# The first batch's q and k requested on GpSimd's queue instead of SyncE's, and zero fills cut to what is read

## The chip, the cores and the metric

The kernel runs on one core of a Trainium2 chip. The core has five engines that work side by side, each with its own instruction stream: TensorE (PE in the profile; its weight loads are listed apart as PEld), VectorE (DVE), ScalarE (ACT), GpSimd (POOL) and SyncE (SP), which only issues transfers here. DMA transfers are requested by an instruction on SP, ACT or POOL and then carried out by 16 DMA engines. In the profile, q1 is the queue of the requests from SP ("hardware_dynamic") and q0 that of the requests from POOL ("software_dynamic").

The metric is the time of one execution on the device in microseconds (us); the median of several runs counts. A profiled execution takes a little longer than an unprofiled one.

## The reference

There are 8 batches, each with 8 heads of 576 positions and 64 features. Linear attention with the feature map phi comes first, then an MLP mixer with a residual (token mixing, then channel mixing):

```
phi(x) = where(x > 0, x, exp(x) - 1) + 1
kv  = phi(k)^T v              (per head, 64 x 64)
z   = sum over positions of phi(k)
x   = phi(q) kv / (phi(q) z + 1e-6)          -> (8, 576, 512)
u   = x + (relu(x^T w_tok1) w_tok2)^T        w_tok1 576x256, w_tok2 256x576
out = u + relu(u w_ch1) w_ch2                w_ch1 512x1536, w_ch2 1536x512
```

All inputs and the output are float32; the kernel computes with bfloat16 operands and float32 sums.

## The kernel before, in words

**Tiling.** The 576 positions of a batch are seen as 64 rows of T = 9 positions. q, k and v of one batch lie on 128 partitions: two groups of 64 rows (heads in two sets), and each of the three tensors is loaded in two halves, `c` = 0 and 1, of two heads per group. One load is 576 KB (128 partitions x 2 x 576 float32). `load` (line 221) makes one such request; batch 1 goes through GpSimd's queue into buffers 1, all other batches through SP's queue into buffers 0. `load_v0` (line 227) loads batch 0's v with a cast to bfloat16 on the way, always on GpSimd's queue, into the space that later holds `cr[1]`.

**Order.** Nothing is left to a scheduler. Each piece of work is a function with a name in the table `tok`, and the long string `ORDER` says in which order the pieces are recorded; that fixes the order on each engine. Semaphores between the engines are derived from which buffers the pieces read and write. The program gives GpSimd's DMAs eight semaphores in turn, so that the ninth waits until the first has landed, and so on.

**The start.** Ahead of `ORDER` stand, from line 1093 on, some instructions that are recorded directly. They are what the change touches:

- DVE fills a zero block (`zeros`, which lies in batch 1's v buffer and feeds the warming matmuls of PE at line 1089) and a one-element tile; ACT runs one exponential on it.
- SP requests the four halves of batch 0's k and q, in the order k0, q0, q1, k1.
- GpSimd makes the identity matrix (for PE's transposes), then zeroes `w1t` (line 1107; the last token weights, of which a half of the partitions is loaded later) and `qT[0]` (line 1108), and requests the two halves of v (recorded at line 230).
- DVE zeroes `kvbd` (line 1106) and `qT[1]` (line 1109), and sets the column of ones in `vs`.
- GpSimd then fills the end of `w2p` (line 1112) and requests the weights: `w1` in two pieces (line 1130), `w1t` (1131), `w2` (1132) and the first two of four blocks of `wc1` (1118). From `ORDER` follow, still on GpSimd, batch 1's k, q and v among the rest of `wc1` and `wc2`.

`qT` holds the transposed phi(q) in blocks of 64 columns. Matrix products read 128 columns at a time from it, so that the last window of a group reaches over 64 columns behind the group's own data; those must hold something finite.

**Batch 0.** For each half: ACT takes the exponential (line 249), DVE x + 1 with a maximum (line 253) and then the minimum of both (line 259), which is phi. PE transposes phi(q) with the identity (line 317), ACT and DVE copy the result into `qT` (line 323), PE multiplies phi(k) with ones (line 561) and with v (line 570), then `qT` with the result (lines 585 and 592), DVE and ACT divide (lines 601 to 616), and PE goes on with the token weights (lines 624 and 635) and with the channel weights (line 683). Warming matmuls (line 1089) stand between the first of these.

**Handing over to batch 1.** Batch 1's v is cast to bfloat16, one half on ACT and one on DVE (line 272), and PE's product of phi(k) and v (line 299) waits for both. From there on the batches run one after another, overlapped, and SP requests the halves of later batches.

The lines that matter most, before the change:

```python
    def load(nm, n, c, gate=None):
        src_ = src[nm][n].rearrange("(j a) (p t) d -> (a p) j (t d)", a=2, t=T)
        js = slice(2 * c, 2 * c + 2)
        queue = nc.gpsimd if n == 1 else nc.sync
        return after(queue.dma_start(out=raw[nm, rb(n)][:, js], in_=src_[:, js]), gate)
```

Of the kernel before, what the change touches and what calls it, by code (L numbers as in the profile page):

```python
# [111 lines left out]
def kernel(  # L112
# [20 lines left out]
    nc = tc.nc  # L133

    B, H, S, D = q.shape
# [5 lines left out]
    T = 2 * R + 1  # L141
# [28 lines left out]
    def const(name, shape, dt=BF16):  # L170
        return consts.tile(shape, dt, name=name, tag=name)

    w1 = const("w1", [128, R, DTOK])
    w1t = const("w1t", [128, 2, DTOK])
# [10 lines left out]
    qT = [const(f"qT{b}", [128, (4 * T + 1) * D]) for b in range(2)]  # L185
# [27 lines left out]
    def after(ins, other):  # L213
        if other is not None:
            tc.add_manual_dep(ins.ins, other.ins.name, sync_dep, reason="order of transfers")
        return ins

    def rb(n):
        return 1 if n == 1 else 0

    def load(nm, n, c, gate=None):
        src_ = src[nm][n].rearrange("(j a) (p t) d -> (a p) j (t d)", a=2, t=T)
        js = slice(2 * c, 2 * c + 2)
        queue = nc.gpsimd if n == 1 else nc.sync
        return after(queue.dma_start(out=raw[nm, rb(n)][:, js], in_=src_[:, js]), gate)

    def load_v0(c):
        src_ = v[0].rearrange("(j a) (p t) d -> (a p) j (t d)", a=2, t=T)
        js = slice(2 * c, 2 * c + 2)
        nc.gpsimd.dma_start(out=v0[:, js].rearrange("p j t d -> p j (t d)"), in_=src_[:, js])  # L230
# [48 lines left out]
    def load_in(nm, n, c):  # L279
        gate = GATE.get(f"{n}{nm}{c}")  # L280
        live["in", nm, n, c] = load(nm, n, c, live[gate] if gate else None)
# [815 lines left out]
    for c, nms in enumerate(("kq", "qk")):  # L1097
        for nm in nms:
            tok[f"0L{nm}{c}"]()
    make_identity(nc, identity)  # L1100
    nc.vector.memset(ones, 0.0)
    for a in range(2):
# [1 line left out]
    nc.vector.memset(vs[:, :, :, D:D1], 1.0)  # L1104
    for b in range(2):
        nc.vector.memset(kvbd[b], 0.0)
    nc.gpsimd.memset(w1t, 0.0)
    nc.gpsimd.memset(qT[0], 0.0)
    nc.vector.memset(qT[1], 0.0)
    for c in range(2):  # L1110
        load_v0(c)
    nc.gpsimd.memset(w2p[:, NT * TD:], 0.0)
    NB = 4
    CB = DCH // NB
# [83 lines left out]
```

## Time and profile before

| | |
|---|---|
| median of 3 runs | 242.99 us (242.88 to 243.49) |
| the profiled execution | 244.04 us, of which the span (first to last instruction) is 242.3 us |
| PE busy | 233.3 us, 96% of the span |
| DVE, ACT, POOL busy | 88%, 56%, 33% |
| granted TensorE clock | 0.999 |
| read from memory, written | 35.85 MB, 9.44 MB |

The page of a profile gives first the busy time of each engine, then the span in 40 equal slices (each digit is the busy share of a slice in tenths), then the DMA queues, and then the chain of work that ended last, followed back from the last instruction. In a timeline row stand start, length, engine, line, operation, output and inputs, and in brackets how long the engine was idle before and what ended the wait. A wait for several semaphores is put down to the one that came last.

### The profile page before, as it was taken

Reading aid. Unit: us, or ns where it says so; the run is one execution under the profiler, and the core shown is the slowest. Engines: PE = TensorE matmul, PEld = TensorE weight load, DVE = VectorE, ACT = ScalarE, POOL = GpSimd, SP = SyncE. Lnnn points to the kernel's source line nnn. Section 1 sums busy time; section 2 is a strip of 40 time slices with the busy share of each in tenths; the row PEclk is TensorE's granted clock in tenths of the full one; section 3 lists DMA queues with packets and bytes.
Section 4 is the critical chain, followed back from the end, with each engine's and each line's share of the span. In section 5 each row is a group of like instructions: output and inputs, shape, how many; then the busy total and the mean of one; then the engine's idle time right before and its main releaser. Section 6 shows DMA issues by size and latency. Waiting matters only on the chain.

```text
span 242.3 us, 6371 instructions
## 1 busy us (share of the span) xinstructions
PE 233.3 (96%) x2616; PEld 174.4 (72%) x2616; DVE 214.0 (88%) x389; ACT 135.7 (56%) x224; POOL 80.8 (33%) x92
## 2 busy tenths in 40 slices
PE   7799999999999999999999999999999999999991
PEld 3485445465678678789777887788678868888880
DVE  5889986999999999999999999999999699867661
ACT  4764781678695287428993496548914442347000
POOL 8684306370800620046000620215014900440730
PEclk9999999999999999999999999999999999999999
DMA  6999999999799988897937989594971285143035
GB/s 237 267 204 302 314 296 303 410 171 307 263 291 175 327 208 156 293 160 259 301 108 162 379 270 182 88 294 156 157 141 25 45 176 108 24 103 70 3 91 170
DMA packets 49037, 48.42 MB, mean 200 GB/s; under 512 B 30064, under 2 KB 35568, under 8 KB 49008
## 3 DMA queue, kind: packets, MB, share of 16 engines
q1 hardware_dynamic: 40032, 31.46, 47.7%
q0 software_dynamic: 8336, 15.76, 28.7%
q10 hardware_dynamic: 640, 0.79, 1.0%
q8 instruction: 20, 0.33, 0.5%
q14 instruction: 9, 0.07, 0.1%
HBM read 35.85 MB, written 9.44 MB: 187 GB/s over the span
## 4 chain that ended last, share of the span: by engine, by line
PE 86%; DMA 8%; DVE 1%; ACT 1%; issue 1%; SPq 1%; ACTq 0%
PE ps L967 26%; PE ps L925 23%; PE ps L445 6%; PE ps L744 5%; DMA v_raw<-in_v_dram 5%; PE ps L456 4%; PE ps L683 4%; DMA k_raw<-in_k_dram 3%; PE ps L708 2%; PE ps L299 2%; PE ps L730 2%; PE ps L1021 2%; PE ps L384 2%; PE ps L624 1%; PE ps L635 1%
## 5 line engine op out<-in xcount | busy, mean ns | idle before, releaser
L967 PE MATMUL ps<-k_raw,v_raw 128*128 128x256 bf16 x252 | 31.5, 273 | 0.0
L940 ACT COPY v_raw<-ps 128x512 f32<-128x512 f32 x30 | 17.2, 593 | 24.1 <-PE ps L925 18.5
L967 PEld LDWEIGHTS <-cr 128*128 128x128 bf16 x252 | 24.5, 98 | 4.8
L967 PEld LDWEIGHTS <-v_raw 128*128 128x128 bf16 x252 | 24.2, 98 | 3.8 <-issue 0.4
L925 PEld LDWEIGHTS <-swc 128*128 128x128 bf16 x240 | 23.3, 98 | 3.5 <-issue 0.4
L925 PEld LDWEIGHTS <-wc 128*128 128x128 bf16 x216 | 21.1, 98 | 4.0
L678 DVE CUSTOM_DVE_ANT_0 cr<-ps,v_raw 128x512 bf16<-128x512 f32 x30 | 20.0, 683 | 4.3 <-PE ps L925 2.1
L925 PE MATMUL ps<-crt,swc 128*128 128x256 bf16 x180 | 23.4, 273 | 0.0
L249 ACT ACTIVATE e<-q_raw 128x1152 bf16<-128x1152 f32 x16 | 18.7, 1167 | 6.7 <-DMA q_raw<-in_q_dram 6.3
L683 PE MATMUL ps<-uT,wc 128*128 128x512 bf16 x96 | 21.9, 379 | 0.0
L967 PE MATMUL ps<-wc,cr 128*128 128x256 bf16 x168 | 21.6, 273 | 0.0
L1068 POOL TENSOR_TENSOR obuf<-obuf,w 128x512 f32<-128x512 f32 x6 | 7.8, 1294 | 40.3 <-DVE obuf L1061 20.2
L249 ACT ACTIVATE e<-k_raw 128x1152 bf16<-128x1152 f32 x16 | 18.6, 1166 | 3.9 <-DMA k_raw<-in_k_dram 3.9
L1068 POOL TENSOR_TENSOR obuf<-obuf,q_raw 128x512 f32<-128x512 f32 x6 | 8.2, 1374 | 35.6 <-DVE obuf L1061 35.6
L925 PE MATMUL ps<-uT,wc 128*128 128x256 bf16 x144 | 19.7, 273 | 0.0
L1061 DVE TENSOR_TENSOR obuf<-ps,u 128x512 f32<-128x512 f32 x24 | 16.3, 684 | 2.7 <-PE ps L967 2.4
L1068 POOL TENSOR_TENSOR obuf<-obuf,part 128x512 f32<-128x512 f32 x6 | 7.7, 1286 | 27.1 <-DVE obuf L1061 27.1
L410 DVE TENSOR_TENSOR x<-ps,dens 128x768 bf16<-128x768 f32 x18 | 16.5, 937 | 0.0
L683 PEld LDWEIGHTS <-wc 128*128 128x128 bf16 x96 | 9.1, 98 | 9.8
L467 DVE TENSOR_TENSOR u<-ps,x 128x1024 bf16<-128x1024 f32 x12 | 14.5, 1218 | 0.1
L833 DVE TENSOR_TENSOR v_raw<-cr 128x512 bf16<-128x512 bf16 (+3 forms) x24 | 14.5, 617 | 0.0
L445 PE MATMUL ps<-x,w 128*128 128x512 bf16 x56 | 14.4, 379 | 0.0
(172 smaller groups left out, 515.1 us busy)
## 6 DMA issues: line engine op xcount, KB each, us to landing
k_raw<-in_k_dram SPq DMA_DIRECT2D x14, 576.0 KB, 6.0
q_raw<-in_q_dram SPq DMA_DIRECT2D x14, 576.0 KB, 5.3
v_raw<-in_v_dram SPq DMA_DIRECT2D x12, 576.0 KB, 6.7
out_dram<-obuf POOLq DMA_DIRECT2D x12, 512.0 KB, 5.7
wc<-in_moe_w_ch_dram POOLq DMA_DIRECT2D x8, 384.0 KB, 11.7
k_raw<-in_k_dram POOLq DMA_DIRECT2D x2, 576.0 KB, 10.0
q_raw<-in_q_dram POOLq DMA_DIRECT2D x2, 576.0 KB, 12.1
v_raw<-in_v_dram POOLq DMA_DIRECT2D x2, 576.0 KB, 11.8
```

Source lines behind the costliest of these rows:

```text
L249: nc.scalar.activation(out=ebuf[EBUF[f"{n}{nm}{c}"]], in_=f, func=AF.Exp)
L410: nc.vector.tensor_tensor(out=xv[:, :, rc0:rc0 + 3], in0=nd_tile(n, m)[:, :, k0:k0 + 6, 0:D].rearrange("p i (q a) d -> p i q a d", a=2), i ...
L445: nc.tensor.matmul(out=banks(f"{n}f")[:, mt], lhsT=w1t[:, b, ms] if r == R else w1[:, r, ms], rhs=x[b][:, r, :], start=(r == 0), stop=(r = ...
L467: nc.vector.tensor_tensor(out=u[b][:, rs], in0=banks(f"{n}g{i}"), in1=x[b][:, rs], op=ALU.add)
L678: nc.vector._custom_dve(TENSOR_ADD_SAT, out=o, in0=ps, in1=c, s0=3.4028234663852886e38, s1=0.0)
L683: nc.tensor.matmul(out=bank(f"{n}m{mc}"), lhsT=wc1[:, kj, 128 * mc:128 * mc + 128], rhs=uTj[b][:, kj] if n < 2 - U1 else uT[b][:, :, kj], ...
L833: return engine.tensor_tensor(out=s_[which - 1][:, ks], in0=x_, in1=y_, op=op)
L925: nc.tensor.matmul(out=ps[:, j], lhsT=lhs[:, k_, 128 * j:128 * (j + 1)], rhs=rhs[:, :, k_], start=(first and j == 0 and k_ == 0), stop=(k_ ...
L940: nc.scalar.copy(out={1: c1, 6: c6, 5: c5}[i], in_=ps)
L967: nc.tensor.matmul(out=ps, lhsT=lhs[:, k_], rhs=rhs[:, k_], start=(first and not skip and k_ == 0), stop=(k_ == KH - 1), skip_group_check= ...
L1061: nc.vector.tensor_tensor(out=slots(f"{n}P", 4)[:, d::2, HC[c]], in0=pair_tile(n, "X" if z == "W" else z), in1=u[n % 2][:, d::2, HC[c]], o ...
L1068: nc.gpsimd.tensor_tensor(out=o, in0=o, in1=part[i], op=ALU.add)
```

## The change

Three things. Batch 0's q and k go through GpSimd's queue, as batch 1's already do, and the two requests for v follow them directly, ahead of the identity matrix and of all fills on GpSimd. The zero fills of `w1t` and `qT` move from GpSimd to DVE, or are cut: of `qT[c]` only the blocks of 64 columns behind the groups that half `c` reads are filled, three blocks in `qT[0]` and two in `qT[1]`, in place of the whole tiles. The string `ORDER` and all orders within it stay.

```diff
@@ -221,7 +221,7 @@
     def load(nm, n, c, gate=None):
         src_ = src[nm][n].rearrange("(j a) (p t) d -> (a p) j (t d)", a=2, t=T)
         js = slice(2 * c, 2 * c + 2)
-        queue = nc.gpsimd if n == 1 else nc.sync
+        queue = nc.gpsimd if n < 2 else nc.sync
         return after(queue.dma_start(out=raw[nm, rb(n)][:, js], in_=src_[:, js]), gate)
 
@@ -1097,6 +1097,8 @@
     for c, nms in enumerate(("kq", "qk")):
         for nm in nms:
             tok[f"0L{nm}{c}"]()
+    for c in range(2):
+        load_v0(c)
     make_identity(nc, identity)
     nc.vector.memset(ones, 0.0)
     for a in range(2):
@@ -1104,11 +1106,10 @@
     nc.vector.memset(vs[:, :, :, D:D1], 1.0)
     for b in range(2):
         nc.vector.memset(kvbd[b], 0.0)
-    nc.gpsimd.memset(w1t, 0.0)
-    nc.gpsimd.memset(qT[0], 0.0)
-    nc.vector.memset(qT[1], 0.0)
+    nc.vector.memset(w1t, 0.0)
     for c in range(2):
-        load_v0(c)
+        for j in sorted({T * c + T, T * (2 + c) + T, 4 * T}):
+            nc.vector.memset(qT[c][:, D * j:D * (j + 1)], 0.0)
     nc.gpsimd.memset(w2p[:, NT * TD:], 0.0)
     NB = 4
     CB = DCH // NB
```

On the engines this gives: SP loses its four first requests. GpSimd's stream begins with six requests (k, q, q, k, v, v), then the identity, the fill of `w2p` and the weights as before. DVE fills `w1t` (256 words of 4 bytes on each partition) and five blocks of 32 such words, in place of one of 1184. GpSimd's requests for `w1t`, `w2` and the first two blocks of `wc1` now have to wait until batch 0's k0, q0, q1 and k1 have landed, because of the eight semaphores. On PE and ACT the order is the same as before.

## The prediction

> **What bounds the kernel now.** I read the page first, then the chain that ended last, then the timeline of the first 13 us, then the DMA queues by window, and last the timeline around 35 us, where the start-up hands over to the steady state.
>
> ```profile
> span 242.3 us, 6371 instructions
> PE 233.3 (96%) x2616; PEld 174.4 (72%) x2616; DVE 214.0 (88%) x389; ACT 135.7 (56%) x224; POOL 80.8 (33%) x92
> PE   7799999999999999999999999999999999999991
> ...
> DMA  6999999999799988897937989594971285143035
> ```
>
> PE is busy in 96% of the span, and only the first two slices of forty (12 us) and the last one show less than nine tenths. The DMA engines (second row) are busy from the first slice to beyond the sixth (36 us) without a pause. The change touches only what happens in the first microseconds. So whatever it does must act on the gaps of the start, and it reaches the end only as far as PE's later work moves with it.
>
> ```profile
> 2.27 8.18 DMA k_raw<-in_k_dram
> ...
> 23.60 11.38 DMA v_raw<-in_v_dram
> ...
> 35.82 0.78 PE ps L299 x71
> ```
>
> These rows of the chain (start, length, what) name two transfers that PE depends on: the fourth load, k's second half, requested at 2.27 and landed 8.18 later at 10.45, and batch 1's v, requested at 23.60 and landed 11.38 later at 34.98. From 35.82 on the chain is nearly all PE. Hence the forecast is a question about two shifts: **y**, how much earlier the compute of the start runs, and **x**, how much earlier batch 1's v lands.
>
> The timeline of the start (start, length, engine, line, what, idle before it and its releaser):
>
> ```profile
> 0.74 0.20 POOL masks.py:197 MEMSET identity<- 128x128 bf16 x1 [0.29 <-POOLq L1182]
> 0.74 0.46 SPq L225 DMA_DIRECT2D k_raw<-in_k_dram  x1
> ...
> 1.26 0.53 POOL L1107 MEMSET w1t<- 128x512 bf16 x1
> ...
> 1.72 2.07 POOL L1108 MEMSET qT<- 128x2368 bf16 x1
> ...
> 3.74 1.71 POOL L230 DMA_DIRECT2D cr<-in_v_dram  x2
> ...
> 4.54 0.76 DVE L253 TENSOR_SCALAR y<-k_raw 128x1152 bf16<-128x1152 f32 x1 [0.83 <-DMA k_raw<-in_k_dram]
> ...
> 8.29 0.68 PE L317 MATMUL ps<-identity,qp 128*128 128x128 bf16 x9 [0.81 <-DVE qp L259]
> ...
> 8.51 1.16 ACT L249 ACTIVATE e<-q_raw 128x1152 bf16<-128x1152 f32 x1 [1.41 <-DMA q_raw<-in_q_dram]
> 8.58 0.96 DVE L253 TENSOR_SCALAR y<-q_raw 128x1152 bf16<-128x1152 f32 x1 [0.35 <-DMA q_raw<-in_q_dram]
> ...
> 10.53 1.16 ACT L249 ACTIVATE e<-k_raw 128x1152 bf16<-128x1152 f32 x1 [0.15 <-DMA k_raw<-in_k_dram]
> ```
>
> ACT and DVE wait for q's second half (ACT 1.41 us, DVE 0.35) and ACT hardly for k's (0.15, because by then it has its own queue of work). A faster fourth load alone is therefore worth almost nothing; what counts is the first load, on which everything stands, and the third.
>
> The next two fences are the DMA queues over 0 to 8 us and over 9.5 to 10.5 us (packets, MB, share). q1 is SP's queue, q0 GpSimd's.
>
> ```profile
> q1 hardware_dynamic: 985, 2.16, 76.6%
> q0 software_dynamic: 1, 0.00, 0.1%
> ```
>
> ```profile
> q0 software_dynamic: 179, 0.19, 113.2%
> q1 hardware_dynamic: 6, 0.01, 2.9%
> ```
>
> This is the decisive view. GpSimd asked for v from 3.74 on, and by 8 us one single packet of q0 had moved, against 2.16 of the 2.36 MB of q and k (four loads of 576 KB). The loads asked for first were served first, across both queues. So q and k are **already ahead of v and the weights**; only the last tenth shares the engines with v, and six stragglers of it come as late as 9.5 to 10.45.
>
> **The change part by part.** (1) Four requests leave SP, at 0.74 to 2.74, and enter POOL ahead of everything else it does after the program's start.
>
> ```profile
> L225 POOL DMA_DIRECT2D k_raw<-in_k_dram x2: 712/720/727, 11.7 to 13.9; - x2
> ```
>
> This row (shortest, median and longest issue in ns, first and last start) is that of batch 1's k: such a load takes 0.72 us to issue on POOL, where SP needs 0.46. The requests then stand at 0.74, 1.46, 2.18 and 2.90, done at 3.62. One load's data take 0.59 MB / 372 GB/s = 1.6 us (rate below), over twice the 0.72 us between requests, so no later request is late; only the first one's way to its first packet counts. For SP, no packet is there by 1.8 us and 15 are by 2.1: 1.06 to 1.36 us after issue. For GpSimd the nearest row is an output store, into an idle q0, at 85.37: none by 86.5 and eleven by 86.7 (the last two fences are windows 0 to 2.1 and 85.3 to 86.7), 1.13 to 1.33 us.
>
> ```profile
> 85.37 1.50 POOL L1072 DMA_DIRECT2D out_dram<-obuf  x2 [2.44 <-issue]
> ```
>
> ```profile
> q1 hardware_dynamic: 15, 0.03, 12.8%
> ```
>
> ```profile
> q0 software_dynamic: 11, 0.05, 13.8%
> ```
>
> The difference lies between -0.23 and +0.27 us. A load's issue shows no other price, and SP's issue ends 0.26 earlier, so I take the start **0.1 later**.
>
> The Trainium skill, page "SBUF — State Buffer", section "SBUF: two separate sides", speaks against this change: while DVE runs an operation in a two-port mode, GpSimd cannot write DMA descriptors, and the transfer starves; it advises the SP or ACT queue instead. The nearest rows here:
>
> ```profile
> 6.53 0.83 DVE L253 TENSOR_SCALAR y<-q_raw 128x1152 bf16<-128x1152 f32 x1
> ...
> 6.75 0.72 POOL L1131 DMA_DIRECT2D w1t<-in_moe_w_tok_dram  x1
> ```
>
> POOL's issue at 6.75 lies almost wholly beside DVE's operation and takes the usual 0.72, so the issue itself shows no stall; whether the transfer did, no row shows, since it was queued behind others. By the rule the sum would end on the slow side (last rival).
>
> (2) The rate. These windows give each stretch's sum, engines, then clock, DMA share and GB/s.
>
> ```profile
> 4.00:8.00 4.00, 3.47 (x6) 1.19 (x4) 2.88 (x4) 2.33 (x2) 4.00 (x7) 1.00 1.02 372
> 30.00:32.00 2.00, 2.00 (x13) 0.90 (x12) 1.86 (x5) 2.00 (x5) 0.00 (x0) 1.00 1.03 417
> 40.00:48.00 8.00, 8.00 (x49) 3.99 (x47) 7.45 (x18) 4.46 (x5) 3.50 (x3) 1.00 1.04 405
> ```
>
> From 4 to 8 us SP's loads run at 372 GB/s, while batch 1's loads on q0 alone reach 417 (30 to 32) and SP's own later ones 405. The gap arises while requests for v and weights are coming in on the second queue. With one queue for all I take the mean of the last two, 411: the 1.49 MB of these 4 us then take 3.63 us, a gain of 0.37. Bounds: 0 (the 372 is the start's own rate) and 0.43 (417). Before 4 us I expect no difference. The stragglers of the fourth load gain up to 0.95 us more (10.45 against 9.5), but ACT waits only 0.15 for them.
>
> (3) v and the weights. v's two issues (0.86 each by the row above) follow at 3.62, ending 5.33, against 5.45 before; identity's fill and select (0.52 from 0.74 to the next start at 1.26) come after them, so it is ready at about 5.9 instead of 1.3, and PE first reads it at 8.29: 2.4 us of cover. w1 is asked for at about 6.0, some 0.5 us later than now. None of that is seen: q0's packets for v and weights wait behind q and k till 8 us anyway. The program gives POOL's DMAs eight semaphores in turn, and a DMA waits until the one eight before it has landed. New waits arise: the request of the w1 tail on k's first half, of w2 on q's first, of two blocks of wc1 on q's second and k's second half. Queued behind them on POOL are the other weights and batch 1's loads. POOL comes to these four at about 7.3, 8.0, 8.7 and 9.5; only the last can wait (until k's second half lands, at most 10.45), and the next request has to wait for v until 11.70 before as after:
>
> ```profile
> 11.70 0.71 POOL L225 DMA_DIRECT2D k_raw<-in_k_dram  x1 [1.86 <-DMA cr<-in_v_dram]
> ```
>
> Cost 0; if the cover were gone, at most the 1 us by which a wc1 block is asked for later, with v and the w1 blocks still queued before it.
>
> (4) The fills. POOL loses 0.53 and 2.07 us, about what the four issues cost (2.88), so its later queue stays 0.5 us behind at most, and is bound by the wait at 11.70. DVE loses a fill and gains others:
>
> ```profile
> 0.92 0.48 DVE L1094 MEMSET v_raw<- 128x512 f32 x1 [0.92 <-PEq L1182]
> ...
> 1.85 0.09 DVE L1104 MEMSET vs<- 128x36 bf16 x1 [0.17 <-issue]
> 1.91 0.56 DVE L1106 MEMSET kvbd<- 128x260 uint32 x2
> 2.66 1.04 DVE L1109 MEMSET qT<- 128x1184 uint32 x1 [0.19 <-issue]
> ```
>
> By its 0.88 ns a word, w1t's 256 words take 0.22; five fills of 32 words take at most 0.09 each, as the 36-element one: 0.67 against 1.04. DVE idles 0.83 us before 4.54 already. Worth 0. SP's next request comes at 36.95, so an emptier SP is worth nothing.
>
> **The sum.** y: everything hangs on the first load, 0.1 later. The third load comes earlier by up to the 0.37, which DVE can use up to its 0.35 of idleness at 8.58. y = 0.35 - 0.1 = about 0.2 (bounds -0.3, if the start is 0.27 late and nothing is gained, and +0.5). x: the DMA stream runs without a pause from the first load to batch 1's v, so its landing moves by 0.37 - 0.1 = 0.27 (bounds -0.27 to 0.66). What PE gains is read at 35 us:
>
> ```profile
> 34.42 1.17 ACT L272 CAST vs<-v_raw 128x1152 bf16<-128x1152 f32 x1
> ...
> 34.90 0.44 PE L317 MATMUL ps<-identity,qp 128*128 128x128 bf16 x5
> 35.00 0.77 DVE L272 CAST vs<-v_raw 128x1152 bf16<-128x1152 f32 x1 [0.66 <-DMA v_raw<-in_v_dram]
> ...
> 35.82 0.78 PE L299 MATMUL ps<-vs,kp 64*64 64x65 bf16 x72 [0.48 <-DVE vs L272]
> ```
>
> PE's k-v product needs both casts. DVE's ends at 35.77 and moves with x. ACT's ends at 35.59, 0.18 earlier; ACT has no idle time here (2.00 of 2.00 us from 30 to 32, and none before this row) and moves with y. PE itself is free at 35.34. So the gain is the smaller of x and y + 0.2: the smaller of 0.27 and 0.4, that is **0.3 us**. If that stall goes, ACT's cast is late next, then PE's own work. After that PE is busy to the end, and nothing takes the gain back or adds to it that I can see.
>
> The profiled execution took 244.04 us with a span of 242.3, and the median of the runs is 242.99, 1.05 less. 244.04 - 0.3 = 243.7 under the profiler, and 242.99 - 0.3 = **242.7** for the median.
>
> **The rivals.**
>
> *Nothing moves.* The words of the change promise q and k ahead of v, and they are ahead already. If 372 GB/s is what this start gives on any queue, x is -0.1 and y -0.1: 243.1. For it: one packet of q0 by 8 us. Against it: 417 on q0 later. The Trainium skill, page "DMA: Bandwidth & Descriptors", section "Queues, rings and completion order", has each engine take turns between its queues packet by packet. By that, v would have shared the engines from about 5 us on and the change would free q and k of it; the 0 to 8 us window disagrees (985 packets against 1), and the turns show only from 8 us on.
>
> *Faster by more than forecast.* The stragglers are a mark that a few of the 16 engines fell behind, and all later landings, batch 1's v too, end with the slowest. If one queue keeps the engines level, x takes in up to 0.95 us besides, and y reaches 0.5 to 0.7 (DVE's 0.35, ACT's 0.15 and up to 0.23 for an earlier first load): the gain is 0.7 to 0.9, 242.2. For it: the six packets after 9.5 us. Against: y + 0.2 caps it, and y needs a start that is not late.
>
> *Slower: the first load's descriptors come late.* POOL's issue is the first thing on that engine, beside DVE's fills, which run from 0.92 to 3.70 before. If the first load lands d later, DVE's 0.35 of idleness hides the first 0.35, and past that each microsecond is one at 35 us, less the 0.2 that ACT has there: it decides from d = about 0.5. Of the fills that DVE has then, the two large ones take 0.48 and 0.56 and those of part (4) 0.67; if they hold up the descriptors, d is 1.0 to 1.7 and the cost 0.5 to 1.2: 243.8 in the middle, 244.2 at the end. For it: no row shows a load on q0 into idle engines. Against it: the 1.13 to 1.33 of the store. The rule of the SBUF page named above gives this case if the fills count among its two-port operations.
>
> **How the numbers follow.** Forecast 0.38, nothing moves 0.24, faster 0.18, slower 0.20. The two in the middle lie within 0.3% (0.73 us, about what a measurement here can tell from no change): same 0.62; faster 0.18, slower 0.20. The range reaches from the middle of the faster case to about the middle of the slower one: 242.0 to 243.9.
>
> **What would show it.** Right: the first exponential on ACT at 4.5 to 4.8; ACT's wait for q's second half under 1.2 us; v's cast on DVE at 34.6 to 34.9; PE's idle time before L299 at 35 us down from 0.48 to 0.2 to 0.4. The forecast is wrong if the first exponential starts past 5.0 (the slow rival), if 4 to 8 us still moves 372 GB/s (nothing moves), or if k's second half lands before 9.5 and v's cast starts before 34.3 (the fast one). A change after 40 us by itself would refute the argument that only the start counts.

## The result and the profile after

| | before | after |
|---|---|---|
| median of 9 runs each, on the same chip | 242.99 us (242.80 to 243.53) | 244.90 us (244.29 to 250.67) |
| ratio after / before | | 1.0076, 95% interval 1.0059 to 1.0094 |
| profiled execution (span) | 244.04 us (242.3) | 245.53 us (243.8) |

The changed kernel is slower by 0.76%, about 1.9 us. Here and below the ratios leave out slowed runs, those more than 1.5% above the fastest of the same kernel: the 250.67 here, and later seven of e3's twelve (248.10 to 249.91), two of e7 (the profiled one among them) and two of e12.

The page of the changed kernel, the rows that answer to those of before (and PE's granted clock, in tenths, per slice of 6.1 us):

```profile
span 243.8 us, 6355 instructions
...
PE   7599999999999999999999999999999999999992
...
PEclk9889999999999999999999999999999999999999
DMA  5999999977989998997948989495792176144026
```

The second slice has fallen from 7 to 5 on PE, the first from 6 to 5 on DMA, and the clock reads 8 in slices two and three, where PE is busy. From the third slice to the last but one PE's row is the same as before. So the loss is to be looked for in the first 18 us.

The start on the time line of the changed kernel (start, length, engine, line, what, and the idle time before it with its releaser):

```profile
1.29 0.86 POOL L225 DMA_DIRECT2D k_raw<-in_k_dram  x1 [0.85 <-POOLq L1183]
2.15 1.43 POOL L225 DMA_DIRECT2D q_raw<-in_q_dram  x2
...
5.25 1.16 ACT L249 ACTIVATE e<-k_raw 128x1152 bf16<-128x1152 f32 x1 [3.02 <-DMA k_raw<-in_k_dram]
8.58 1.16 ACT L249 ACTIVATE e<-q_raw 128x1152 bf16<-128x1152 f32 x1 [2.16 <-DMA q_raw<-in_q_dram]
...
10.59 1.14 PE L317 MATMUL ps<-identity,qp 128*128 128x128 bf16 x9 [2.67 <-DVE qp L259]
...
38.09 0.78 PE L299 MATMUL ps<-vs,kp 64*64 64x65 bf16 x72
```

Three things went another way than the prediction had them. GpSimd's first request starts at 1.29, not at 0.74: its sequencer (POOLq) takes 0.85 us first. The exponential of k0 starts at 5.25 instead of 4.54. And that of q0, which started right behind it before, now comes 3.3 us later:

```profile
5.94 1.17 ACT L249 ACTIVATE e<-q_raw 128x1152 bf16<-128x1152 f32 x1 [0.23 <-DMA q_raw<-in_q_dram]
```

That is the row of the kernel before: 5.94 against 8.58, so of q0's 2.64 us only 0.71 come with k0; the rest is q0's own. The chain of the changed kernel names it as the first long link, requested at 2.15 and landed 6.40 later:

```profile
2.15 6.40 DMA q_raw<-in_q_dram
```

The first packet lies between 2.8 and 2.9: the queues from 0 to 2.8 us show no packet, and those from 0 to 2.9 this.

```profile
q0 software_dynamic: 5, 0.02, 4.1%
```

And the windows of the changed kernel (stretch, its sum, engines, then granted clock, DMA share, GB/s) show why q0 is late, and what follows from that:

```profile
4.00:8.00 4.00, 3.92 (x6) 1.35 (x4) 1.79 (x2) 1.16 (x1) 3.92 (x7) 1.00 0.91 303
...
6.00:7.00 1.00, 1.00 (x3) 0.48 (x2) 0.84 (x2) 0.42 (x1) 0.93 (x2) 1.00 0.74 184
...
11.00:12.00 1.00, 1.00 (x17) 1.00 (x16) 1.00 (x3) 0.38 (x2) 0.36 (x2) 0.50 1.20 196
```

From 6 to 7 us the stream runs at half its pace, 184 GB/s, in the midst of q0's data; from 4 to 8 us it moves 303 GB/s where the kernel before had 372. After PE's wait of 2.67 us the granted clock is 0.50. (PE's row for L317 shows the same by its length: nine transposes take 1.14 us, against 0.68 before.)

How the delay of 2.30 us at L317 (8.29 to 10.59) reaches the end is read in one stretch, from L317 to L299. First the kernel before, then the one after:

```profile
8.29:35.82 27.53, 26.02 (x283) 16.13 (x284) 24.11 (x45) 20.15 (x40) 12.48 (x17) 1.00 1.20 271
```

```profile
10.59:38.09 27.50, 26.84 (x281) 17.50 (x284) 23.86 (x44) 19.34 (x40) 11.91 (x17) 0.94 1.20 270
```

The stretch is equally long, but differently filled. Before, PE had 27.53 - 26.02 = 1.51 us of idle time in it, 0.48 of them ahead of L299. After, 0.66 are left: 0.85 us of the delay is made good. But PE's same work takes 26.84 instead of 26.02, as the clock is at 0.94 of its full rate on average. The one pays for the other, and L299 starts 2.27 us later. From L299's start to the end of the profiled execution it is 208.22 us before and 207.44 after, so that in these two profiles 0.78 us of the 2.27 are made good behind L299. In the profiles of all seventeen kernels of this study that rest lies between 207.3 and 208.4, while L299 itself starts anywhere from 35.09 to 44.01. So the large differences arise ahead of L299; what happens behind it moves the time by 1.1 us at most. (Before's profiled execution was 1.05 us above its median, after's 0.63, and e6's 0.09 below: a profiled execution is not always the longer one. Differences between profiles are good for places, the medians for sizes.)

### The profile page after: what moved, and what is told of

Read it like the earlier page. It is cut to its first block, busy times and chain, and to the rows that moved or that the text cites. A ratio compares the mean times of both kernels' runs of the same rounds, so it can differ in the third digit from the quotient of the medians.

```text
span 243.8 us, 6355 instructions
## 1 busy us (share of the span) xinstructions
PE 233.5 (96%) x2598; PEld 175.7 (72%) x2616; DVE 213.5 (88%) x394; ACT 135.7 (56%) x224; POOL 81.6 (33%) x94
## 4 chain that ended last, share of the span: by engine, by line
PE 92%; DMA 3%; ACT 1%; issue 1%; DVE 1%; POOL 0%; DVEq 0%; POOLq 0%
PE ps L967 26%; PE ps L925 23%; PE ps L683 8%; PE ps L744 6%; PE ps L445 6%; PE ps L456 4%; DMA q_raw<-in_q_dram 3%; PE ps L708 2%; PE ps L730 2%; PE ps L299 2%; PE ps L1021 2%; PE ps L384 2%; PE ps L317 1%; PE ps L1089 1%; PE ps L624 1%
## 5 line engine op out<-in xcount | busy, mean ns | idle before, releaser
L253 DVE TENSOR_SCALAR y<-k_raw 128x1152 bf16<-128x1152 f32 x16 | 12.7, 794 | 2.4 <-DMA k_raw<-in_k_dram 2.3
```

## The experiments

The theory after the result: the start on GpSimd's queue itself is late, by a late first packet, by a slow stretch in q0's data, and by the clock that falls while PE waits. The rivals for the first runs: that the moved fills and the identity's later place cost the time, or that v's requests, now closer behind q and k, take the engines from them. Where the expectations use letters, A is that theory, B and C are the two rivals in this order. Fifteen kernels were run; a table of the starts of eight of them, beside before and after, comes first, as the sections refer to it. Exponential of k0 and q0 (ACT), L317 (PE) and L299 (PE) are start times in the profile, GB/s is that of 6 to 7 us, the ratio is to the kernel before on the same chip.

| kernel | k0 | q0 | 6 to 7 us, GB/s | L317 | L299 | profiled us | ratio |
|---|---|---|---|---|---|---|---|
| before | 4.54 | 5.94 | 369 | 8.29 | 35.82 | 244.04 | 1 |
| after | 5.25 | 8.58 | 184 | 10.59 | 38.09 | 245.53 | 1.0076 |
| e2, only the queue | 5.62 | 8.23 | 189 | 10.54 | 39.90 | 247.49 | 1.0124 |
| e3, all but the queue | 4.56 | 5.95 | 280 | 8.41 | 36.66 | 244.37 | 1.0075 |
| e10, first halves on SP | 4.65 | 6.23 | 415 | 8.44 | 35.09 | 243.31 | 0.9974 |
| e11, k0 alone on SP | 4.28 | 8.39 | 350 | 10.40 | 37.85 | 245.19 | 1.0049 |
| e6, before, SP late | 5.63 | 7.06 | 359 | 9.51 | 36.44 | 244.49 | 1.0054 |
| e9, identity first | 5.76 | 7.22 | 318 | 9.49 | 37.11 | 244.50 | 1.0049 |
| e12, before, q0 third | 4.40 | 8.20 | 378 | 10.21 | 36.40 | 244.41 | 1.0086 |
| e5, after, nine warming | 5.38 | 7.83 | 230 | 11.18 | 37.21 | 244.79 | 1.0061 |

### Which part of the change costs: e2, e3

**e2: the kernel before with the queue's line alone.**

```diff
-        queue = nc.gpsimd if n == 1 else nc.sync
+        queue = nc.gpsimd if n < 2 else nc.sync
```

> The kernel before, with only batch 0's q and k moved to GpSimd's queue; identity, fills and v's requests stay where they were on GpSimd, behind the four requests, so v is asked for about 3 us later than in the kernel after. Theory A (the queue by itself brings q late): the first exponential starts at about 5.25, that of q's first half after 7, the time is 1.5 to 2.5 us above before. Rival C (v's casting requests, issued from 4.3 to 5.7 in the kernel after, are what holds up q's packets from 5.15 to 8 us): q's first half lands at about 6.7, 0.7 later than before like the first load, and the time is 0.3 to 1.0 us above before. Rival B (the moved identity and fills make the loss): the time is that of before or up to 0.3 above.

Measured: 246.04 us, ratio 1.0124 (1.0097 to 1.0151). The start shows all of the changed kernel's marks, and GpSimd's fills stand between k1's request and v's:

```profile
1.30 0.86 POOL L225 DMA_DIRECT2D k_raw<-in_k_dram  x1 [0.85 <-POOLq L1182]
...
5.27 2.07 POOL L1108 MEMSET qT<- 128x2368 bf16 x1
7.29 0.81 POOL L230 DMA_DIRECT2D cr<-in_v_dram  x1
```

The request at 1.30, k0 at 5.62, 189 GB/s from 6 to 7 us, q0 at 8.23: the queue alone does all that. v was asked for only at 7.29, so v's requests can't be what made q0 late. Both rivals fall as the cause of the late start. The changed kernel is 1.2 us faster than e2 (1.0124 to 1.0076), but two things are mixed in that. The fills no longer stand ahead of v on GpSimd, and in e2's profile L299 waits 0.72 us for DVE's cast of batch 1's v. And the clock was low for longer, from before 10 us until after 16, so that PE's same work from L317 to L299 took 28.11 us against 26.84:

```profile
10.54:39.90 29.36, 28.11 (x283) 18.28 (x284) 24.83 (x45) 19.26 (x40) 15.90 (x21) 0.90 1.20 263
```

The runs don't part the two.

**e3: the changed kernel with q and k back on SP.**

```diff
-        queue = nc.gpsimd if n < 2 else nc.sync
+        queue = nc.gpsimd if n == 1 else nc.sync
```

> The kernel after, with q and k back on SP's queue; the fills stay cut and v is the first thing that GpSimd asks for, at about 0.8 to 1.3 us. Theory A: the loss goes with the queue; but v's packets now come among those of q and k, because requests are served in the order in which they come in, so q's second half and k's second half land up to 3 us later, and the time is 0.5 to 1.5 us above before. Rival B (the moved identity and fills make the loss): the time stays at that of the kernel after, 1.9 above before, with the first loads landing as early as before. Rival C: q's packets stall as in the kernel after, from about 1 us after v's requests on.

Measured: ratio 1.0075 (1.0039 to 1.0111), from four runs at 244.37 to 244.57 and one at 247.84; by the four alone it is 1.05 to 1.25 us over before's 243.32. So the rest of the change costs about a microsecond when q and k are on SP's queue. The reason that the profile shows is a new one: v is now asked for at 1.27, ahead of q1, and from 5 to 8 us the two queues move about the same number of packets.

```profile
q0 software_dynamic: 271, 0.30, 58.9%
q1 hardware_dynamic: 256, 0.55, 53.0%
```

k0 and q0 come on time (5.95), but q1 has to share with v, and its exponential starts at 9.65, where it started at 8.51 before. In the kernel before GpSimd's fills (2.60 us by the rows of the prediction) held v's requests back until SP had asked for all four. They did a job that no line of the program names.

### What the change would be worth with a start on time: e10, e11

**e10: k0 and q0 on SP, q1 and k1 on GpSimd ahead of v.** Everything else as in the changed kernel.

```diff
-        queue = nc.gpsimd if n < 2 else nc.sync
+        queue = nc.gpsimd if n == 1 or (n == 0 and c == 1) else nc.sync
```

> The changed kernel with the first halves, k0 and q0, asked for on SP, and only q1 and k1 on GpSimd ahead of v. If the loss comes from the late first load and from q0's late last packets on GpSimd's queue: first exponential at 4.5 to 4.6, q0's at about 5.95, PE's wait ahead of L317 under 1 us, clock 1.00, time within 0.4 us of the kernel before (0.9985 to 1.0015). If the loss comes from what stands behind the loads (v and the weights asked for earlier, the fills on DVE), it stays: about 1.0075, as with all four on SP.

Measured: 242.53 us against 243.23, ratio 0.9974 (0.9963 to 0.9985): faster than both kernels, by 0.26% than before, which is more than expected, and by 1.0% than after (0.9974 / 1.0076). Its rows:

```profile
1.29 0.86 POOL L225 DMA_DIRECT2D q_raw<-in_q_dram  x1 [0.85 <-POOLq L1183]
...
6.23 1.17 ACT L249 ACTIVATE e<-q_raw 128x1152 bf16<-128x1152 f32 x1 [0.42 <-DMA q_raw<-in_q_dram]
...
8.44 0.68 PE L317 MATMUL ps<-identity,qp 128*128 128x128 bf16 x9 [0.51 <-DVE qp L259]
...
35.09 0.78 PE L299 MATMUL ps<-vs,kp 64*64 64x65 bf16 x72
```

```profile
4.00:8.00 4.00, 3.93 (x6) 1.35 (x4) 2.84 (x4) 2.65 (x3) 3.65 (x9) 1.00 1.03 410
```

GpSimd's first request is as late as before, at 1.29, but SP's two loads cover it. There is no slow stretch, PE doesn't lose its clock, and the wait of 0.48 us ahead of L299 is gone, since batch 1's v comes earlier: DVE's cast of it starts at 34.11 instead of 35.00. 410 GB/s from 4 to 8 us is the rate that the prediction had put down for one queue (411). So what lay behind the loads in the change (v and weights directly behind, short fills) costs nothing here; the loss came from the first halves' queue.

**e11: only k0 on SP.** It takes away the late first load and leaves q0 to GpSimd.

```diff
-        queue = nc.gpsimd if n < 2 else nc.sync
+        queue = nc.sync if n > 1 or (n, nm, c) == (0, "k", 0) else nc.gpsimd
```

> The changed kernel with the first load alone, k0, on SP; q0, q1 and k1 on GpSimd. It takes away the late start and leaves q0 on GpSimd's queue. If the late start is the larger part: first exponential at 4.55, q0's at 6 to 7 (its request at 1.3 is still early enough), time within 0.5 us of the kernel before (1.000 to 1.002). If the stream on GpSimd's queue halves at 6 to 7 us wherever the first load is, q0's exponential comes at 7.5 to 8.5, PE waits over 2 us ahead of L317, and the time is 1.003 to 1.006.

Measured: 244.67 us, ratio 1.0049 (1.0032 to 1.0065). k0 comes at 4.28, and q0 nevertheless at 8.39. The windows of e11:

```profile
4.00:5.00 1.00, 1.00 (x2) 0.34 (x1) 0.72 (x1) 0.72 (x1) 1.00 (x2) 1.00 1.01 212
5.00:6.00 1.00, 1.00 (x3) 0.45 (x2) 0.56 (x2) 0.44 (x1) 0.93 (x3) 1.00 0.77 194
6.00:7.00 1.00, 1.00 (x3) 0.43 (x2) 0.23 (x1) 0.00 (x0) 1.00 (x3) 1.00 0.95 350
```

The slow stretch has moved with q0: it begins at 4 us, as soon as k0 is done and q0's packets start. So it is a delay of its own, beside the late start. The twelve runs fall apart: three at 243.34 to 243.62 with a clock of 0.997 or 0.998, eight at 244.55 to 245.19 with 0.991 to 0.993, and one at 244.54 with 0.999. Only one was profiled, of the slower kind; whether the three had no slow stretch, or only no fall of the clock, was not seen.

### What a late start costs by itself: e6, e9, e12

**e6: the kernel before, with SP's first request held back to 1.70 us.** DVE's short fills of `ones` move ahead and SP's first load waits for the last of them.

```diff
+    nc.vector.memset(ones, 0.0)
+    for a in range(2):
+        late = nc.vector.memset(ones[half[a], a:a + 1], 1.0)
     for c, nms in enumerate(("kq", "qk")):
         for nm in nms:
             tok[f"0L{nm}{c}"]()
+            if (nm, c) == ("k", 0):
+                after(live["in", "k", 0, 0], late)
```

> The kernel before with SP's first request made to wait for one of DVE's fills, so that q and k are asked for on SP's queue about 1.0 us late (at about 1.75 in place of 0.74) and their first packet moves at about 2.9, as on GpSimd's queue, while nothing else changes. Theory A1 (the late start is the whole of the loss): first exponential at 5.5, the exponential of q's first half at 7.0, time 1.5 to 2 us above before. Theory A2 (the late start is the smaller part; what counts is that GpSimd's queue then loses speed between 5.5 and 8 us, so that q's first half takes 1.6 us more): q's exponential at 6.9 to 7.1 and the time 0.6 to 1.1 us above before.

Measured: 244.58 us, ratio 1.0054 (1.0039 to 1.0069), 1.3 us. By 2.9 us six packets have moved, about as in the changed kernel (five). PE:

```profile
9.51 0.68 PE L317 MATMUL ps<-identity,qp 128*128 128x128 bf16 x9 [2.57 <-DVE qp L259]
```

All comes later by the same amount: k0's exponential by 1.09, q0's by 1.12, L317 by 1.22. Nothing of it is hidden up to there, and the median is later by as much, between the ranges of A1 and A2. Without a slow stretch and with full clock (0.68 us for the nine transposes), the late first packet alone makes 1.3 us of the 1.9. e6 is a fair stand-in for that: k0's exponential at 5.63 lies among the 5.21 to 5.66 of the seven profiles with all four loads at the head of GpSimd's queue and k0 first on ACT. The profile bears out the place of the delay, but not its whole size:

```profile
9.51:36.44 26.93, 25.69 (x283) 16.29 (x284) 23.56 (x44) 19.28 (x40) 10.77 (x16) 1.00 1.20 275
```

From L317 to L299 it is 0.60 us shorter than before's 27.53, so that L299 comes only 0.62 later, and the profiled execution is 0.45 longer. As before's profiled execution lay 1.05 above its median, the 1.3 rests on the medians alone.

**e9: the changed kernel with the identity made ahead of the loads**, all four still on GpSimd.

```diff
+    make_identity(nc, identity)
     for c, nms in enumerate(("kq", "qk")):
```

> The changed kernel with the identity's fill and select ahead of the four loads on GpSimd. In the changed kernel GpSimd's first request starts at 1.29 us, after 0.85 us of its sequencer's own preparation, and the first packet moves at 2.87. If that preparation runs beside the engine's other work, the fill and the select (0.52 us) hide in it: request at about 1.3, first exponential at about 5.25, time as the changed kernel's (1.0076 of the kernel before). If the preparation belongs to the request and begins only when GpSimd comes to it: request at 1.8 or later, first exponential at about 5.75, time 0.3 to 0.6 us above the changed kernel's (1.009 to 1.010).

Measured: 244.42 us, ratio 1.0049 (1.0031 to 1.0068), below both expectations and below the changed kernel's 1.0076, though the two intervals overlap. GpSimd's rows:

```profile
0.74 0.20 POOL masks.py:197 MEMSET identity<- 128x128 bf16 x1 [0.29 <-POOLq L1183]
1.02 0.29 POOL masks.py:199 TENSOR_SCALAR_AFFINE_SELECT identity<-identity 128x128 bf16<-128x128 bf16 x1
1.49 0.86 POOL L225 DMA_DIRECT2D k_raw<-in_k_dram  x1 [0.18 <-issue]
```

The fill starts at 0.74, where the request couldn't, and the request only 0.20 later than without it: most of the 0.55 us that GpSimd spends ahead of its first request runs beside other work. In this execution the slow stretch is weak, if there is one (318 GB/s from 6 to 7 us; the kernel before has 332 from 5 to 6), q0's exponential comes at 7.22, and the time is about e6's. So two kernels with a start some 1.2 us late, one on each queue, come out at 1.2 and 1.3 us. The agreement is rough: in e9's profiled execution the clock fell as well (the nine transposes took 1.11 us), and its two runs with a clock of 1.0 took 244.20 and 244.34, 1.0 and 1.1 over.

**e12: the kernel before, requests in the order k0, q1, q0, k1.** Only q0 is late.

```diff
-    for c, nms in enumerate(("kq", "qk")):
-        for nm in nms:
-            tok[f"0L{nm}{c}"]()
+    for w in ("k0", "q1", "q0", "k1"):
+        tok[f"0L{w}"]()
```

> The kernel before with its four requests on SP in the order k0, q1, q0, k1 (before: k0, q0, q1, k1): q0 comes third, some 1.5 to 2.5 us later, and nothing else moves. It prices a late q0 by itself, with the first load on time. q0's exponential at 7.2 to 8.5 (before 5.94), PE's wait ahead of L317 2 to 3 us, clock down after it if the idle time does that. If PE's late start behind q0 reaches the end: 0.8 to 1.5 us longer (1.003 to 1.006). If the gap at 35 us takes it back (0.48 us of PE's idle time and what lies behind it): 1.000 to 1.002.

Measured: ratio 1.0086 (1.0055 to 1.0117), in two groups: five runs at 243.78 to 244.67 (clock 0.996 to 1.0), three at 246.32 to 246.94 (0.990 to 0.992). A late q0 alone costs 0.6 to 1.4 us over 243.23 in the first group, and 3 us and more in the second, where the clock is lower. Only the first group was profiled; what makes the 2 us between them is not seen. Late k0 and late q0 don't add up: both make the same L317 late (9.51 in e6, 10.21 here, 10.59 with both).

### What the clock costs: e1, e4, e5

**e1 and e5: the changed kernel with six and with nine warming products** ahead of L317 in place of four.

```diff
-    first = [lambda: tok["0kx0"](), lambda: tok["0ka0"](), lambda: warm(0, 4),
+    first = [lambda: tok["0kx0"](), lambda: tok["0ka0"](), lambda: warm(0, 6),
```

> The kernel after, with six instead of four matmuls in the first warming group (PE busy to about 10.5 us). Theory A (q's first half lands 2.6 us late on GpSimd's queue; the drop of PE's granted clock to 0.5 between 10 and 13.6 us is a result of the 2.7 us in which PE has nothing to do, and a price of its own): the clock stays at 1.00, PE's transposes still start at about 10.6, and the time falls by 0.4 to 0.8 us below that of the kernel after, not further. Rival (the clock is nearly all of the loss): it falls by 1.5 us or more, to that of the kernel before. Rival (the clock falls for another reason than idleness): it still reads 0.5 and the time does not move.

Measured: 245.19 us, 1.0081 (1.0060 to 1.0103). Six products ended at 8.71, PE still idled 1.68 us, and against expectation the clock still fell, here from 12 us on:

```profile
10.39 0.68 PE L317 MATMUL ps<-identity,qp 128*128 128x128 bf16 x9 [1.68 <-DVE qp L259]
```

```profile
12.00:15.00 3.00, 3.00 (x52) 2.04 (x51) 1.80 (x3) 1.75 (x2) 1.49 (x3) 0.50 1.33 199
```

The run says nothing of the price. With nine:

> The kernel after with nine matmuls in the first warming group. With six the group ended at 8.7 us and the clock still fell, after 1.7 us of idleness; nine should end at about 10, so that under 0.7 us are left before the transposes at 10.4 to 10.6. Theory A (late data first, the clock a price of its own on top): the granted clock stays at 1.00 from 10 to 14 us, the transposes of q's second half come about 1 us earlier than in the kernel after, and the time is 0.5 to 1.0 us below it, so 1.0 to 1.4 us above before. Rival (the clock's price is absorbed by the wait for batch 1's v): clock 1.00, but the time stays within 0.3 us of the kernel after. Rival (the clock is all of it): the time is that of before.

Measured: 244.71 us, 1.0061 (1.0047 to 1.0075). PE has no idle time ahead of L317, which starts 0.59 later than in the changed kernel because the last products are in its way; and yet L299 starts 0.88 earlier:

```profile
11.18:37.21 26.03, 25.53 (x283) 16.28 (x281) 23.24 (x43) 18.75 (x39) 11.43 (x16) 1.00 1.21 274
```

The same work takes PE 25.53 us at full clock, against 26.84 in the changed kernel: 1.3 us. The kernel before took 26.02 at full clock, so 0.8 to 1.3 us of PE's time is the price of a fall like the changed kernel's. In the medians the gain is smaller and not certain (1.0061 against 1.0076, with overlapping intervals), as the clock doesn't fall in all executions: of the changed kernel's eight runs four with clocks of 0.995 to 1.0 took 244.29 to 244.78, four with 0.991 to 0.993 took 244.90 to 246.26. So 1.3 to 1.8 us over 242.99 are there even where no fall is on record.

**e4: the kernel before with two warming products in place of four.**

```diff
-    first = [lambda: tok["0kx0"](), lambda: tok["0ka0"](), lambda: warm(0, 4),
+    first = [lambda: tok["0kx0"](), lambda: tok["0ka0"](), lambda: warm(0, 2),
```

> The kernel before, with two instead of four matmuls in the first warming group, so that PE has nothing to do from about 4.5 to 8.3 us while no transfer is touched. It prices the clock by itself. Theory A: the granted clock falls to 0.5 for about 3 us from 8 us on, and the time rises by 0.4 to 0.8 us. Rival (the clock is nearly all of the loss): it rises by 1.5 us or more. Rival (idleness does not lower the clock): nothing changes, clock 1.00.

Measured: 244.22 us, 1.0042 (1.0029 to 1.0055). L317 starts at 8.25, on time, with the clock down, and L299 at 35.82, exactly as before: here the wait for batch 1's v takes the whole price back in the profile. The runs with the clock at 0.989 to 0.991 (243.54 to 244.68) aren't slower than those at 0.998 to 1.0 (244.07 to 244.81). What these 1.0 us are, then, I can't say. The recorded clock doesn't account for them, but it can read too high (e14 below), so the clock isn't ruled out.

### Why the stream slows in q0: e7, e8, e13, e14, e15

**e7: the changed kernel with q0's exponential and phi ahead of k0's** on ACT and DVE, so that nothing reads SBUF for phi before 7.9 us (only the order of the names in `ORDER` is changed).

```diff
-ORDER = """A2 A0 A1 A3 A4 A5 A6 A8 A9 ...
+ORDER = """A2 A4 A5 A6 A0 A1 A3 A8 A9 ...
```

> The kernel after with phi of q's first half ahead of phi of k's first half on ACT and DVE, so that neither engine reads anything between the landing of k (5.3) and that of q. It asks whether their reading is what slows the transfers between 5.2 and 8 us. If so: 6 to 7 us moves at 350 GB/s or more, and q's first half lands at about 6.9. If not: 6 to 7 us stays below 250 GB/s and q's exponential starts at 8.2 to 8.6 as before this edit; phi of k then comes later and the time is up to 1 us above the kernel after.

Measured: ratio 1.0152 (1.0131 to 1.0172), from two runs at 246.74 and 247.26, more than the 1 us above the changed kernel that was expected. 217 GB/s from 6 to 7 us, with ACT and DVE idle and the clock at 1.00 up to 10 us: their reads are not the cause.

**e8: v's first request waits until q1 has landed**, so that GpSimd does nothing from 4.3 us on.

```diff
-        load_v0(c)
+        after(load_v0(c), live["in", "q", 0, 1] if c == 0 else None)
```

> The kernel after with v's first request held back until q's second half has landed, so that GpSimd does nothing between 4.3 us and about 9 to 10 us: no further requests, no fills, no identity. It asks whether GpSimd's own work slows the transfers between 5.2 and 8 us. If so: 6 to 7 us moves at 350 GB/s or more and q's exponential starts near 7. If the slowness belongs to the queue itself: 6 to 7 us stays below 250 GB/s and q's exponential starts at 8.2 to 8.6. The time is well above the kernel after in both cases, as v, identity and weights come later.

Measured, in one run: 247.60 us (PE waits for the identity, which now comes late). 235 GB/s from 6 to 7 us beside an idle GpSimd: its own later work isn't the cause. Against expectation q0 got through just ahead of it here (exponential at 7.00), so that the stretch doesn't belong to q0's data.

**e13: DVE's fills of `vs`, `kvbd`, `w1t` and `qT` held back until k0 has landed.** This is the trial of the prediction's slow rival.

```diff
-    nc.vector.memset(vs[:, :, :, D:D1], 1.0)
+    after(nc.vector.memset(vs[:, :, :, D:D1], 1.0), live["in", "k", 0, 0])
```

> The changed kernel with DVE's fills of vs, kvbd, w1t and qT held back until k0 has landed; nothing runs on DVE between 1.7 and 5 us, while GpSimd asks for its loads. If DVE's fills hold up what GpSimd writes for a load: first packet at 2.4 to 2.6 (after: 2.87), k0 landed at 4.8 or so, and no packets of over 1 us at 5 to 8 us, q0 landed by 6.9. If they don't: first packet at 2.85 to 2.9, k0 landed at 5.2, and 5 to 8 us as in the changed kernel. DVE's phi of k0 is late by the fills, some 1.2 us, in both.

Measured, in one run: 244.76 us. DVE did nothing from 1.67 to 5.61:

```profile
1.51 0.16 DVE L1105 MEMSET ones<- 64x1 bf16 x2
5.61 0.09 DVE L1106 MEMSET vs<- 128x36 bf16 x1 [3.94 <-DMA k_raw<-in_k_dram]
```

And the queues from 0 to 2.9 us:

```profile
q0 software_dynamic: 5, 0.02, 6.2%
```

Five packets by 2.9 with the fills or without, and 230 GB/s from 6 to 7 us: DVE's fills cause neither the late first packet nor the slow stretch.

**e14: one warming product in place of four** ahead of L317; PE reads nothing from 3.5 us on.

```diff
-    first = [lambda: tok["0kx0"](), lambda: tok["0ka0"](), lambda: warm(0, 4),
+    first = [lambda: tok["0kx0"](), lambda: tok["0ka0"](), lambda: warm(0, 1),
```

> The changed kernel with one warming product in place of four ahead of L317: PE reads nothing from 3 to 10 us, where it read v_raw until 7.9. If PE's reads slow the writes of the loads: no packets of over 1 us from 5 to 8 us, 350 GB/s or more at 6 to 7, q0 landed by 7.1. If they don't: 184 to 250 GB/s at 6 to 7 us and q0 at 7.8 to 8.6 as before. PE's clock falls after the idle time in both, so the time is at or above the changed kernel's.

Measured, in one run: 245.95 us; 235 GB/s from 6 to 7 us and q0's exponential at 8.10. PE's reads aren't the cause either. The row of L317 is worth a look:

```profile
10.11 1.14 PE L317 MATMUL ps<-identity,qp 128*128 128x128 bf16 x9 [6.57 <-DVE qp L259]
```

Nine transposes in 1.14 us are the slow clock (0.68 is the full one), though the clock column says 1.00 in all windows of this execution. The length of a known row is the safer witness.

**e15: the mirror of e10**, k0 and q0 on GpSimd, q1 and k1 on SP.

```diff
-        queue = nc.gpsimd if n < 2 else nc.sync
+        queue = nc.gpsimd if n == 1 or (n == 0 and c == 0) else nc.sync
```

> The mirror of the split: k0 and q0 on GpSimd, q1 and k1 on SP. SP asks at 0.74 and 1.2, so q1 and k1 come first and k0 and q0 share or follow. If only the order of requests counts, k0 lands third at 6 to 7.5 us, q0 at 7.5 to 9, and the time is 1.010 or more of the kernel before. If the slow stretch belongs to GpSimd's queue in these microseconds, SP's loads run at 370 GB/s and GpSimd's at 180 to 250 behind them, q0 past 8.5. If the slow stretch needs all four on GpSimd, the queues together run at 370 or more throughout.

Measured: 248.54 us, 1.0229 (1.0204 to 1.0254). As k0 and q0 come third and fourth, it starts far too late (k0 at 8.11). But the same two loads on GpSimd's queue now run at full pace:

```profile
6.00:7.00 1.00, 1.00 (x3) 0.19 (x1) 0.00 (x0) 0.00 (x0) 1.00 (x3) 1.00 1.04 419
7.00:8.00 1.00, 0.16 (x1) 0.00 (x0) 0.00 (x0) 0.00 (x0) 0.37 (x1) 1.00 1.04 422
```

So GpSimd's queue isn't slow as such, nor are q0's data. The slow stretch was there in every profile in which GpSimd carried three or four loads of the start (in e9 at most weakly: 318), and not in e10 and e15, where it carried two behind SP's two. Whether the number of loads counts or their place in the order, these runs don't part, and the cause stays open. What it costs differs from execution to execution: with all four loads on GpSimd's queue, q0's exponential starts between 7.00 (e8) and 8.58, and the changed kernel's profile shows the latest of them.

## Why the prediction was wrong, point by point

- **Only the start counts, through L317, L299 and the gap at 35 us:** right in the main. From L299 to the end it takes 207.3 to 208.4 us in all profiles; that nothing behind it takes anything back doesn't hold to better than these 1.1 us.
- **(1) The start, 0.1 us later:** this is the step that failed first. It put the first request at 0.74, where GpSimd's first instruction had stood; a request there starts at 1.29, after 0.85 us of POOLq instead of 0.29. And it took the way to the first packet from a store late in the run (1.13 to 1.33 us); here it is 1.51 to 1.61 (e9: 1.41 to 1.61). Together the first packet comes 0.7 to 1.1 us later (none by 2.8 against none by 1.8, five by 2.9 against fifteen by 2.1), not -0.23 to +0.27. e6 prices that at 1.3 us, e9 at 1.2. The Trainium skill, page "DMA: Bandwidth & Descriptors", section "Latency and other measured facts", gives about 1 us to the first byte for GpSimd's path and 0.6 for SP's; from the start of the request both take longer here (1.51 to 1.61, and SP's 1.06 to 1.36), while the difference of 0.4 fits the rows. The 0.55 ahead of the request is in no row of before.
- **(2) The rate, 411 in place of 372 GB/s from 4 to 8 us:** wrong for the change (303), right for e10 (410), where also the rest of the step holds: batch 1's v earlier, the 0.48 us ahead of L299 gone, 0.26% gained where 0.3 us (0.12%) had been forecast. The term failed because the stream on GpSimd's queue had a slow stretch in the first loads that no row of before could show; what remains of the 1.9 us after the late first packet, 0.6 us, falls to it and to the clock together. The runs don't part these two safely.
- **The clock** stands in no step. In the kernel before PE waits 0.81 us ahead of L317; in the changed one it waits 2.67 and the clock falls for about 3 us, worth 0.8 to 1.3 us of PE's time in an execution in which it happens. The Trainium skill, page "TensorE: Matmul & The Clock Gate", section "What's actually happening", has the clock decided by a free-running window of some 3.4 us, so that equal kernels differ from run to run; the two groups of e11's and e12's runs fit that. Idle times shorter than that window were enough here, 1.68 us in e1 and 2.67 in the changed kernel, while 2.57 and 3.01 in e6 and e12 did nothing in their profiled executions.
- **(3) v and the weights, 0:** the identity and the weights, as costed, weren't waited for. But the step overlooked what GpSimd's fills did for the order: without them v's requests overtake SP's q1 (e3, 1.0075). In the change itself the common queue prevents that.
- **(4) The fills, 0:** with the requests on GpSimd, taking them away is a gain. Between e2 and the changed kernel lie 1.2 us, as v is asked for at 4.27 instead of 7.29 and the clock was low for longer in e2's profile; how much is the fills' isn't shown.
- **The rivals.** *Slower* had the sign, and at its end, 244.2, still lay 0.7 us short. Its point of decision was wrong: it let the first 0.35 us hide in DVE's idle time and 0.2 more at 35 us. In e6 nothing is hidden ahead of L317, because the later loads stand behind the first one and come late with it; 0.60 us between L317 and L299 in its profile is not in its median. Its mechanism is refuted by e13. The Trainium skill's rule that it leaned on (page "SBUF — State Buffer", section "SBUF: two separate sides": DVE's two-port operations keep GpSimd from writing descriptors) isn't seen in these fills. *Nothing moves* took the rate of the start to be the same on any queue; e10's 410 and the changed kernel's 303 from 4 to 8 us speak against it. *Faster* is nearest to what e10 does (v's cast earlier by 0.9 us, 0.26% gained), but not on the queue that the change chose.
- **What would show it** named the right row: the first exponential past 5.0 us.

## What to carry to other kernels

The first load of a kernel is on the critical path with everything behind it: keep it, and the one that PE needs next, on the queue whose first request is quickest, and give the slower queue what comes third. Requests that are already in the right order still get their order from something; look for what holds the later ones back (here two long fills) before taking it away. And a price taken from the middle of a run (a store's issue) isn't one for the first instruction of a program.

## What was not expected of the hardware

- GpSimd's first request takes 0.85 us of its sequencer, the first fill 0.29; with the fill and a select ahead, the request is only 0.20 us later (1.49 against 1.29).
- The stream of four loads on GpSimd's queue falls to about half for a microsecond around 6 us (184 to 235 GB/s from 6 to 7 us in eight profiles), whichever of ACT and DVE, PE or GpSimd was left idle; with k0 on SP (e11) it comes from 4 to 6 us (212 and 194).
- Two queues moved about equal numbers of packets where the second queue's request came in ahead of the first's (e3, v's ahead of q1's: 271 packets against 256 from 5 to 8 us), and the second hardly any where it came in after (the prediction's 1 against 985).
- The granted clock can read 1.00 in every window while the rows show a slow clock (e14: 1.14 us for what takes 0.68).
